# Attention scores on half the array's rows: two heads' products side by side, and one store of seven PSUM banks

## The chip, the core and the metric

The kernel runs on one core of a Trainium2 chip. The engines are PE (matrix products; PEld is its weight load), DVE (vector), ACT (scalar functions), POOL (general) and SP (issues the transfers). PE multiplies through an array of 128 rows and 128 columns: a weight block lies in the array, and the moving operand's columns stream through it. PE writes only to PSUM, which has eight banks of 512 float32 columns for each of 128 partitions; DVE and ACT read it from there. The metric is the device time of one execution in microseconds (us).

## What is computed

One transformer block, 2048 positions, width 512: a layer norm modulated by a conditioning vector, attention with 32 heads of 16 in a causal window of 256, a gated residual, a second layer norm, and a gated feed-forward part of 1792.

```python
def _A_ref(x, wqkv, wo):
    H = 32; Dh = D // H; W = 256
    ...
    scores = jnp.einsum("bhqd,bhkd->bhqk", q, k) * (Dh ** -0.5)
    mask = (idx[:, None] - idx[None, :] >= 0) & (idx[:, None] - idx[None, :] < W)
    scores = jnp.where(mask[None, None], scores, -1e9)
    p = _softmax(scores, axis=-1)
    o = jnp.einsum("bhqk,bhkd->bhqd", p, v)
    return (lambda x, *d: x.transpose(*d))(o, 0, 2, 1, 3).reshape(B, S, D) @ wo
...
h = _layernorm(x, axis=-1) * (1 + ca) + sa
x = x + ga * _A_ref(h, A_wqkv, A_wo)
h = _layernorm(x, axis=-1) * (1 + cb) + sb
x = x + gb * _B_ref(h, B_w1, B_w3, B_w2)
```

## The kernel before

Attention is cut into 32 units: 8 groups of four heads times 4 blocks of 512 positions. Unit u goes through three stages, which run at the same time for different units.

- `unit_a` (L429) projects queries and keys: 12 products of 512 columns into one bank (L438), two copies out of it on ACT (L444, L447), the rest on POOL (L451), and then SP spreads the rows into two rings, `ringk` and `ringq` (L457, L459). Numbers are kept in two parts, a coarse float32r one and its remainder, so that a head has 3 x 16 = 48 rows.
- `unit_b` (L475) finds each query's greatest score: a product (L485), then on DVE a mask and a maximum in one instruction (L494), which a short instruction follows that reads the result out. The negated maxima, again in two parts (L502, L503), are turned on PE (L509), copied by ACT (L514) and stored by SP as two more rows of `ringq` (L517), so that the score products subtract them.
- `unit_c` (L724) computes the scores transposed, keys by queries (L752), masks them, takes exponentials on ACT into `pt`, and multiplies by the values (L720): four heads side by side, each in a quarter of the array's columns, into the bank `po`. The result is copied out (L814) and stored.

The score products go two heads at a time (`a` counts the pairs of a unit). A pair's two heads stand one below the other in 96 rows, and `ringq` holds zeros in the other head's rows, so that a product keeps the heads apart by its columns: the maximum's products take 64 queries of both heads against up to 320 keys (L485), the scores' products 128 keys against both heads' 256 queries of the two near blocks, and one more of 256 columns for the far block (L752). The edges of the window are masked in one of four ways, by a letter for each of the eight score blocks of a unit in `MODE` (`MODL` for the last three units): C merges the two edge blocks on DVE (L772), so that one exponential serves both and POOL cuts the halves apart (L779); D adds masks on DVE (L760); P copies the edges to SBUF on ACT (L784), masks them on POOL (L794) and takes the exponentials from there (L786, L798); E adds the masks by a product on PE (L755).

PSUM's banks are dealt out by name: three `mx` (maxima, turns), three `st` (scores), one `pj` (projections), one `po`.

The order of all instructions up to the time `TS` is fixed by the table `X`: each operation of a unit has a place in it, units are 8 apart, and `at` collects them to be sorted. Each engine carries out its instructions in that order and waits where an operand or a bank is not ready. From `TS` on the same list is mixed with the output projection's and the feed-forward part's operations by `Sched.deal` (L150). A prologue does the first norm, the values, three units' `unit_a` and two units' `unit_b` by the table `Y`.

## Time and profile before

| | us |
|---|---|
| median of 3 runs (lowest, highest) | 968.09 (966.83, 968.49) |
| the profiled execution | 967.35 |
| its span, first to last instruction | 965.6 |
| PE busy | 921.7 (95%) |
| DVE busy | 672.0 (70%) |
| ACT busy | 524.8 (54%) |
| POOL busy | 544.1 (56%) |

The span is 1.75 us shorter than the execution's time. The mean granted TensorE clock is 0.988. Busy shares are means over stages that are limited in different ways; views by stretch and by line are needed to read a change in one stage. A matmul's record reaches from its issue to its modelled end, and neighbours overlap, so what one costs PE is the distance between starts, not its length.

### The profile page before, as it was taken

How to read it: one execution, taken by the hardware profiler on the slowest of the kernel's cores; microseconds unless marked ns; L12 is line 12 of the kernel's file. 1: busy time of each engine (PE TensorE's matmuls, PEld its weight loads, DVE VectorE, ACT ScalarE, POOL GpSimd, SP SyncE). 2: the span in 40 equal slices, each digit the busy share in tenths (PEclk: the TensorE clock that was granted, in tenths of full speed). 3: DMA queues.
4: the chain of work that ended last, by engine and by line, in shares of the span. 5: the costliest groups of instructions: out<-in, count | busy, mean ns of one | idle time of the engine just before them, and what ended most of it. 6: DMA issues, size and time to landing. Idle time of an engine off the chain costs nothing.

```text
span 965.6 us, 16735 instructions
## 1 busy us (share of the span) xinstructions
PE 921.7 (95%) x5330; PEld 708.9 (73%) x5330; DVE 672.0 (70%) x1864; ACT 524.8 (54%) x1031; POOL 544.1 (56%) x691
## 2 busy tenths in 40 slices
PE   5999999999999999978987999999999999999998
PEld 2678677777777777755665878888888888888886
DVE  7575689898898989876568555675569645565455
ACT  3333677787877777764677654333455334433330
POOL 5221465676656665643665689986657446443420
...
GB/s 307 174 87 46 105 186 163 153 149 163 183 170 139 163 160 149 138 181 183 247 218 1 206 222 312 215 184 162 77 166 149 182 42 95 98 65 92 25 22 87
DMA packets 125020, 141.62 MB, mean 147 GB/s; under 512 B 60034, under 2 KB 72834, under 8 KB 124932
## 3 DMA queue, kind: packets, MB, share of 16 engines
...
q10 hardware_dynamic: 720, 1.05, 0.3%
...
## 4 chain that ended last, share of the span: by engine, by line
PE 82%; DVE 7%; ACT 3%; DMA 3%; issue 3%; SPq 1%; POOL 1%; DVEq 0%; POOLq 0%; ACTq 0%
PE mx L1375 12%; PE st L1375 12%; PE pj L438 9%; PE st L752 8%; PE mx L485 8%; PE po L720 8%; PE st L1468 7%; PE mx L1468 7%; PE pj L1375 4%; PE st L652 2%; PE pj L1468 2%; PE st L1113 1%; PE mx L1113 1%; DVE junk L494 1%; DMA wo<-wsum 1%
## 5 line engine op out<-in xcount | busy, mean ns | idle before, releaser
L494 DVE CUSTOM_DVE_ANT_0 junk<-mx,mskq 128x320 bf16<-128x320 f32 (+4 forms) x512 | 223.0, 465 | 37.9 <-PE mx L485 37.1
L967 POOL TENSOR_TENSOR w<-w,w 128x512 fp32r<-128x512 f32 (+2 forms) x56 | 106.8, 1924 | 117.5 <-ACT w L966 99.0
L485 PE MATMUL mx<-ringk,ringq 96*128 96x320 f32 (+4 forms) x512 | 153.8, 324 | 5.5 <-DMA ringq<-qk 3.0
L752 PE MATMUL st<-ringq,ringk 98*128 98x256 f32 (+1 forms) x528 | 141.4, 336 | 7.1 <-DVE st L772 3.1
L779 POOL TENSOR_SCALAR_AFFINE_SELECT pt<-pt 128x256 f32<-128x256 f32 x224 | 92.4, 412 | 88.3 <-ACT pt L767 80.7
L438 PE MATMUL pj<-hT,wq 128*128 128x512 f32 x384 | 132.3, 402 | 1.8 <-ACT wq L423 1.0
L485 PEld LDWEIGHTS mx<-ringk,ringq 96*128 96x128 f32 x512 | 97.8, 192 | 44.5 <-DVE mt L494 21.4
L767 ACT ACTIVATE pt<-st 128x512 f32<-128x512 f32 (+1 forms) x198 | 115.8, 587 | 25.9 <-DVE st L760 7.7
L752 PEld LDWEIGHTS st<-ringq,ringk 98*128 98x128 f32 x528 | 91.1, 193 | 22.0 <-ACT pt L767 5.4
L720 PE MATMUL po<-pt,vS 128*17 128x384 f32 (+2 forms) x1408 | 92.5, 392 | 2.8 <-ACT pt L767 1.5
L438 PEld LDWEIGHTS pj<-hT,wq 128*128 128x128 f32 x384 | 68.3, 191 | 10.2 <-ACT wq L423 1.4
L1375 PE MATMUL mx<-b,w 128*128 128x512 f32 x264 | 68.2, 397 | 6.0 <-ACT t L1409 5.7
L1406 DVE TENSOR_TENSOR t<-mx,t 128x512 f32<-128x512 f32 x48 | 33.0, 689 | 45.3 <-PE mx L1375 22.6
L1406 DVE TENSOR_TENSOR t<-st,t 128x512 f32<-128x512 f32 x48 | 33.1, 690 | 44.7 <-PE st L1375 25.0
L720 PEld LDWEIGHTS po<-pt,vS 128*17 128x17 f32 x1408 | 34.8, 98 | 39.4 <-issue 19.9
L1375 PEld LDWEIGHTS mx<-b,w 128*128 128x128 f32 x264 | 50.1, 191 | 17.2 <-ACT t L1409 6.0
L1446 ACT ACTIVATE wq<-g 128x512 fp32r<-128x512 f32 x28 | 17.7, 631 | 81.6 <-DVE g L1402 33.6
L772 DVE COPY_PREDICATED st<-later,st 128x256 f32<-128x256 uint8 x112 | 47.4, 423 | 18.7 <-PE st L752 16.2
L1375 PE MATMUL st<-b,w 128*128 128x512 f32 x240 | 60.3, 390 | 0.0
L794 POOL TENSOR_SCALAR_AFFINE_SELECT sm<-sm 128x256 f32<-128x256 f32 x109 | 42.6, 409 | 28.7 <-ACT sm L784 27.7
L760 DVE TENSOR_TENSOR st<-st,mskr 128x256 f32<-128x256 f32 x125 | 53.6, 429 | 7.0 <-PE st L752 5.8
L451 POOL TENSOR_TENSOR qk<-qkr,qk 128x512 fp32r<-128x512 f32 x32 | 42.2, 1320 | 25.8 <-ACT qk L447 25.8
...
## 6 DMA issues: line engine op xcount, KB each, us to landing
...
ringq<-qk SPq DMA_DIRECT2D x192, 64.0 KB
...
```

Source lines behind the costliest of these rows:

```text
L438: nc.tensor.matmul(v["ps"], WQ[g][w][:, n // 3], hTp(i, n // 3, b * BT, BT), start=(n == 0), stop=(n == 3 * KC - 1))
L485: nc.tensor.matmul(v[i][:, :n], both_queries(a, gs), keys(NS, a, (gs + 1) * HP - n, n), start=True, stop=True)
L494: nc.vector.tensor_tensor_reduce(out=junk[:, :n], in0=v[i][:, :n], in1=mskq[:, WK - n:], scale=1.0, scalar=-3e38, op0=ALU.add, op1=ALU.max ...
L720: nc.tensor.matmul(po[32 * i:32 * i + DH + 1, qb * P:(qb + nq) * P], vS[:, kb, 4 * g + i], pts[i // 2][:, i % 2, c0:c0 + nq], start=first, ...
L752: nc.tensor.matmul(o, keys(NM, a, kb * P, P), queries(a, q, n), start=q == lo, stop=not plus and q + n == hi, skip_group_check=True)
L760: nc.vector.tensor_tensor(out=ps, in0=ps, in1=mskk[:, p:p + 1].to_broadcast([P, 2, P]), op=ALU.add)
L767: nc.scalar.activation(held[u, j, a][:, :, :n], v[j, a, 0].rearrange("p (h q) k -> p h q k", h=2)[:, :, :n], AF.Exp, scale=SCALE)
L779: nc.gpsimd.affine_select(out=pt[:, :, 2 * m], in_=pt[:, :, 0], **w)
L967: sch.op(eng, lambda: on_eng(eng).tensor_tensor(out=lo(), in0=src(), in1=hi().bitcast(F32), op=ALU.subtract), 0.06 + 0.0024 * n if eng == ...
L1375: nc.tensor.matmul(ps(bk), WT[s, n][w][:, col], BB[t, k][r], start=start and c == 0, stop=stop and c == 5, skip_group_check=True)
L1406: return nc.vector.tensor_add(o, x, y)
L1468: nc.tensor.matmul(ps(bk), tiles[hk + (h,)][:, i * P:(i + 1) * P], w2_of(last, y, f), start=(m == 0), stop=(m == 5))
```

## The change

Each head now has 64 rows of the rings to itself: one head of a pair lies in rows 0 to 63 of the array, the other in rows 64 to 127. A product of one head uses its 64 rows alone, and each product of old becomes two, one for each half, which write to two banks. The maximum's product takes 128 queries of one head against up to 384 keys (L497 of the new kernel), the scores' product 128 keys against up to 384 queries, near and far blocks in one (L764). The maximum's row comes to lie at rows 31, 63, 95 and 127, where the key ring holds ones; since these rows take part in the maximum's product, zeros are written there first (`zrow`). Masks, merges and exponentials work on one head and all its blocks (`hh` counts the heads), where they worked on two heads and one or two blocks. `MODE` drops D, gains one P and one E, whose masking products become an operation of their own (`plus`, L773). The named banks `mx`, `st` and `pj` become one store of seven, `take` handing out the one that was given back first. The table `X`, and with it the whole order, is new.

```diff
-WK = 5 * HP
-X = dict(oa=-3.863, ob=1.029, wqk=(-0.858, 1.939, 10.434), pj=(0.286, 0.344, 0.878, 1.131, 3.631, 3.672,
-         3.878, 4.077, 4.364, 4.951, 5.551, 5.743), ev=(7.049, 6.063), mix=(8.982,), row=(9.561, 6.099, 6.443,
-         6.374, 9.289, 9.261, 10.681, 9.981, 10.464), mx=(6.98, 5.852, 5.041, 5.414, 2.887, 8.92, 4.178, 7.678,
-         8.523, 4.734, 2.476, 7.344, 4.677, 8.087, 3.397, 9.325), tl=(0.121, 1.116, 0.068, 0.241, 0.054, 0.054,
-         0.03, 0.054, 0.03, 0.429, 0.101, 0.086, 0.03, 0.03, 0.03, 0.03), mr=(10.275, 10.832, 11.16, 11.231),
-         st=(2.246, 2.098, 4.353, 2.468, 3.726, 3.854, 5.37, 5.955, 6.87, 6.701, 5.531, 6.783, 8.785, 8.433,
-         8.729, 8.272), c1=(0.082, 0.03, 0.03, 0.03, 0.58, 0.083, 0.104, 0.452), c2=(0.996, 0.977, 1.143, 0.243,
-         0.033, 0.569, 0.983, 0.032), c3=(0.25, 6.673, 0.348, 1.207, 1.713, 0.316, 0.385, 1.653), pv=(6.434,
-         10.575, 10.975, 11.087, 6.249, 6.261), o=(11.83, 12.324), job=(0.275, 3.004, 9.681), gate=7.93)
+WK = 3 * P
...
-MODE = 'CDCPCDCP'
...
+MODE = 'CPCPCPCE'
...
-MXB = 3
-STB = 3
-MODL = 'CECECECE'
+XN = 7
+MODL = 'CPCPCPCE'
 NL = 3
 XB = 6
-PTB = 9
+PTB = 12
...
+    free, gone, left = list(range(XN)), [], {}
+    def take(uses=1):
+        i = free.pop(0)
+        left[i] = uses
+        return i, psA.tile([P, BT], F32, name=f"x{i}", bufs=1)
+    def done(bank, give=0):
+        i = bank[0]
+        left[i] -= 1
+        if left[i] == 0:
+            if give or left.get("give"):
+                left["give"] = left.get("give", 0) + give - 1
+                gone.append(i)
+            else:
+                free.append(i)
...
-    ringq = ap.tile([P, NB, 2, 8, 2, HP], F32R, name="ringq")
-    NS, NM = 6 * DH, 6 * DH + 2
-    def queries(a, qb, n):
-        b, i = divmod(qb, 4)
-        return ringq[:NM, b, a, 2 * i:2 * (i + n)].rearrange("p s h t -> p h s t")
-    def both_queries(a, qs):
-        return ringq[:NS, qs // 8, a, qs % 8].rearrange("p h t -> p (h t)")
-    def keys(rows, a, lo, n):
-        return ringk[:rows, a, lo:lo + n]
+    ringq = ap.tile([P, 2, S], F32R, name="ringq")
+    zrow = ap.tile([4, 2, BT], F32, name="zrow")
+    nc.gpsimd.memset(zrow, 0.0)
+    sel = ap.tile([P, 5], F32, name="sel")
+    nc.gpsimd.memset(sel, 0.0)
+    nc.gpsimd.affine_select(out=sel[:, :4], in_=sel[:, :4], pattern=[[-32, 4]], base=-31, channel_multiplier=1,
+                            compare_op=ALU.not_equal, fill=1.0)
+    def hrow(ring, hh, a, lo, n):
+        return ring[HP * hh:HP * hh + HP, a, lo:lo + n]
...
-            (r, low), n = ((((0, 0), 0), ((1, 2), 0), ((2, 1), 1))[n // 3], n % 3)
-            raw = v[low].bitcast(F32)
-            if n == 0:
-                nc.sync.dma_start(ringk.bitcast(F32)[r[0]:NS:3, :, b * BT:(b + 1) * BT], raw[:HP])
-            else:
-                nc.sync.dma_start(
-                    ringq.bitcast(F32)[NS // 2 * (n - 1) + r[1]:NS // 2 * n:3, b, :, :, n - 1].rearrange(
-                        "p a s t -> p (a s) t"),
-                    raw[HP + 32 * (n - 1):HP + 32 * n])
+            if n == 6:
+                nc.sync.dma_start(ringq.bitcast(F32)[31::32, :, b * BT:(b + 1) * BT], zrow)
+                return
+            (r, low), n = ((((0, 0), 0), ((1, 2), 0), ((2, 1), 1))[n // 2], n % 2)
+            ring = (ringk, ringq)[n].bitcast(F32)
+            nc.sync.dma_start(ring[r[n]::4, :, b * BT:(b + 1) * BT], v[low].bitcast(F32)[HP * n:HP * n + HP])
...
-            qs, a = divmod(i, 2)
-            gs = 8 * b + qs
-            n = min(5, gs + 1) * HP
-            v[i] = psA.tile([P, BT], F32, name="mx", bufs=MXB)
-            nc.tensor.matmul(v[i][:, :n], both_queries(a, gs), keys(NS, a, (gs + 1) * HP - n, n),
-                             start=True, stop=True)
-        def top(i):
-            qs, a = divmod(i, 2)
-            n = min(5, 8 * b + qs + 1) * HP
+            qb, a = divmod(i, 2)
+            q = 4 * b + qb
+            n = min(3, q + 1) * P
+            for hh in range(2):
+                v[i, hh] = take()
+                nc.tensor.matmul(v[i, hh][1][:, :n], hrow(ringq, hh, a, q * P, P),
+                                 hrow(ringk, hh, a, (q + 1) * P - n, n), start=True, stop=True)
+        def top(i, hh):
+            qb, a = divmod(i, 2)
+            n = min(3, 4 * b + qb + 1) * P
             if "mt" not in v:
-                v["mt"] = a1.tile([P, 2, 8], F32, name="mt", bufs=2)
+                v["mt"] = a1.tile([P, 4, 4], F32, name="mt", bufs=2)
             junk = a1.tile([P, WK], BF16, name="junk", bufs=2)
             nc.vector.tensor_tensor_reduce(
-                out=junk[:, :n], in0=v[i][:, :n], in1=mskq[:, WK - n:], scale=1.0, scalar=-3e38,
-                op0=ALU.add, op1=ALU.max, accum_out=v["mt"][:, a, qs:qs + 1])
+                out=junk[:, :n], in0=v[i, hh][1][:, :n], in1=mskq[:, WK - n:], scale=1.0, scalar=-3e38,
+                op0=ALU.add, op1=ALU.max, accum_out=v["mt"][:, 2 * a + hh, qb:qb + 1])
+            done(v[i, hh])
...
+        def rows(a):
+            nc.sync.dma_start(ringq.bitcast(F32)[31::32, a, b * BT:(b + 1) * BT], v["mT"][16 * a:16 * a + 16])
...
-        def bank(j, a, p):
-            ps = v[j, a, p]
-            return ps.rearrange("p (h q) k -> p h q k", h=2)[:, :, 0] if p == 0 else ps[:, :2]
-        def scores(j, a, p):
-            kb = 4 * b + j
+        def scores(j, a):
+            kb, n = 4 * b + j, blocks(j)
             if (u, j, a) not in held:
                 held[u, j, a] = a2.tile([P, 2, 3, P], F32, name="pt", bufs=PTB)
-            v[j, a, p] = ps = psA.tile([P, 4, P], F32, name="st", bufs=STB)
-            plus = mode(j, a) == "E"
-            lo, hi = (kb, kb + min(2, blocks(j))) if p == 0 else (kb + 2, kb + 3)
-            both = [(lo, hi - lo)] if lo // 4 == (hi - 1) // 4 else [(lo, 1), (hi - 1, 1)]
-            for q, n in both:
-                o = ps.rearrange("p (h q) k -> p h q k", h=2)[:, :, q - lo:q - lo + n] if p == 0 else ps[:, :2]
-                nc.tensor.matmul(o, keys(NM, a, kb * P, P), queries(a, q, n), start=q == lo,
-                                 stop=not plus and q + n == hi, skip_group_check=True)
-            if plus:
-                nc.tensor.matmul(bank(j, a, p), identr, mskr[:, p:p + 1].to_broadcast([P, 2, P]), start=False,
+            for hh in range(2):
+                v[j, a, "b", hh] = take()
+                v[j, a, hh] = ps = v[j, a, "b", hh][1].rearrange("p (q k) -> p q k", k=P)
+                nc.tensor.matmul(ps[:, :n].rearrange("p q k -> p (q k)"), hrow(ringk, hh, a, kb * P, P),
+                                 hrow(ringq, hh, a, kb * P, n * P), start=True,
+                                 stop=mode(j, a) != "E", skip_group_check=True)
+        def edge(t, j):
+            return t[:, 0:3:2] if blocks(j) == 3 else t[:, :1]
+        def plus(j, a):
+            for hh in range(2):
+                nc.tensor.matmul(edge(v[j, a, hh], j), identr, mskr[:, :2 if blocks(j) == 3 else 1], start=False,
                                  stop=True, skip_group_check=True)
-        def mask(j, a, p):
-            ps = bank(j, a, p)
-            nc.vector.tensor_tensor(out=ps, in0=ps, in1=mskk[:, p:p + 1].to_broadcast([P, 2, P]), op=ALU.add)
-        def probs(j, a, p):
-            n = min(2, blocks(j))
-            if p:
-                nc.scalar.activation(held[u, j, a][:, :, 2], bank(j, a, 1), AF.Exp, scale=SCALE)
-            else:
-                nc.scalar.activation(held[u, j, a][:, :, :n], v[j, a, 0].rearrange(
-                    "p (h q) k -> p h q k", h=2)[:, :, :n], AF.Exp, scale=SCALE)
-        def merge(j, a):
-            nc.vector.copy_predicated(bank(j, a, 0), later, bank(j, a, 1))
+        def mask(j, a, hh):
+            ps = edge(v[j, a, hh], j)
+            nc.vector.tensor_tensor(out=ps, in0=ps, in1=mskk[:, :2 if blocks(j) == 3 else 1], op=ALU.add)
+        def probs(j, a, hh):
+            n = 2 if mode(j, a) == "C" else blocks(j)
+            nc.scalar.activation(held[u, j, a][:, hh, :n], v[j, a, hh][:, :n], AF.Exp, scale=SCALE)
+            done(v[j, a, "b", hh])
+        def merge(j, a, hh):
+            ps = v[j, a, hh]
+            nc.vector.copy_predicated(ps[:, 0], later, ps[:, 2])
...
-        def side(j, a, p):
+        def side(j, a, hh):
             if (j, a, "m") not in v:
-                v[j, a, "m"] = a2.tile([P, 2, 2, P], F32, name="sm", bufs=1)
-            nc.scalar.activation(v[j, a, "m"][:, :, p], bank(j, a, p), AF.Copy)
-            if p == 0 and blocks(j) > 1:
-                nc.scalar.activation(held[u, j, a][:, :, 1], v[j, a, 0].rearrange(
-                    "p (h q) k -> p h q k", h=2)[:, :, 1], AF.Exp, scale=SCALE)
+                v[j, a, "m"] = a2.tile([P, 2, 2, P], F32, name="sm", bufs=2)
+            ps = v[j, a, hh]
+            nc.scalar.activation(v[j, a, "m"][:, hh, :2 if blocks(j) == 3 else 1], edge(ps, j), AF.Copy)
+            if blocks(j) > 1:
+                nc.scalar.activation(held[u, j, a][:, hh, 1], ps[:, 1], AF.Exp, scale=SCALE)
+            done(v[j, a, "b", hh])
```

PE's order in the middle of the attention loop, before: rows of one unit, from a visit of the value products (L720) on; L485 is a maximum's product, L752 a score's, L438 a projection's, L509 the turn.

```order
L720 MATMUL po<-pt,vS 17x384 x4
L720 MATMUL po<-pt,vS 17x256 x4
L720 MATMUL po<-pt,vS 17x128 x4
L485 MATMUL mx<-ringk,ringq 128x320
L752 MATMUL st<-ringq,ringk 128x512
L752 MATMUL st<-ringq,ringk 128x256
L509 MATMUL mx<-ident,mr 32x128
L485 MATMUL mx<-ringk,ringq 128x320
L752 MATMUL st<-ringq,ringk 128x512
L438 MATMUL pj<-hT,wq_2190 128x512
L485 MATMUL mx<-ringk,ringq 128x320
L438 MATMUL pj<-hT,wq_2190 128x512
```

The same place in the new order, with the numbers of banks and tiles; L497 is a maximum's product on half the rows, L764 a score's, L773 the masking product of mode E, L451 a projection's, L740 a value product.

```order
L497 MATMUL x2_2304<-ringk_103,ringq_104 128x384
L497 MATMUL x6_2306<-ringk_103,ringq_104 128x384
L764 MATMUL x4_2309<-ringq_104,ringk_103 128x384
L764 MATMUL x1_2311<-ringq_104,ringk_103 128x384
L773 MATMUL x4_2309<-mskr_129,identr_130 128x2x128
L773 MATMUL x1_2311<-mskr_129,identr_130 128x2x128
L451 MATMUL x0_2291<-hT_95,wq00_1509 128x512
L497 MATMUL x3_2319<-ringk_103,ringq_104 128x384
L497 MATMUL x5_2321<-ringk_103,ringq_104 128x384
L740 MATMUL po_99<-pt_2165,vS_101 17x384 x2
L740 MATMUL po_99<-pt_2223,vS_101 17x384 x2
L497 MATMUL x2_2330<-ringk_103,ringq_104 128x384
```

Before, products on the whole array stood one behind the other, and the value products' quarters came in long visits; now pairs on half the rows stand between single whole-array products and short visits.

DVE's order in the loop, before: L494 is the maximum (and the row that reads it out), L772 a merge, L760 a mask.

```order
L494 ISA junk_5365,mt_5364<-mx_5360,mskq_105 128x320
L494 ISA mt_5364 128x1
L772 COPY_PREDICATED st_5368<-later_127,st_5372 128x2x128
L494 ISA junk_5379,mt_5364<-mx_5377,mskq_105 128x320
L494 ISA mt_5364 128x1
L760 TENSOR_TENSOR st_5385<-st_5385,mskr_128 128x2x128
L494 ISA junk_5392,mt_5364<-mx_5390,mskq_105 128x320
```

And now, where L506 is the maximum and L788 a merge:

```order
L506 ISA junk_5762,mt_5723<-x2_5758,mskq_112 128x384
L506 ISA mt_5723 128x1
L506 ISA junk_5764,mt_5723<-x0_5760,mskq_112 128x384
L506 ISA mt_5723 128x1
L788 COPY_PREDICATED x5_5782<-later_128,x5_5782 128x128
L506 ISA junk_5814,mt_5723<-x1_5786,mskq_112 128x384
L506 ISA mt_5723 128x1
L788 COPY_PREDICATED x6_5784<-later_128,x6_5784 128x128
```

The maxima grew from 320 to 384 columns, a merge of two heads became two of one head, and the masks are gone from this place.

157 lines of the change are left out of this document (90 added, 67 removed).

## The prediction

> **What bounds the kernel now.** The first view is the busy time of each engine in stretches of the span (columns: microseconds of the stretch, then busy time of PE, PE's weight loads, DVE, ACT and POOL, the granted clock, the DMA share). The rows are the attention loop, the tail in which attention runs out under the output projection, and most of the feed-forward part; a prologue lies ahead.
>
> ```profile
> core 0 of [0], span 965.6 us
> ...
> 136.00:414.00 278.00, 276.30 (x2249) 204.14 (x2241) 246.84 (x1043) 212.08 (x485) 178.27 (x347) 1.00 0.60 156
> 414.00:480.00 66.00, 55.21 (x370) 36.66 (x362) 41.80 (x118) 36.33 (x78) 31.89 (x47) 0.92 0.73 202
> ...
> 520.00:966.00 446.00, 439.85 (x1910) 357.20 (x1910) 261.84 (x366) 182.76 (x290) 253.86 (x190) 0.99 0.40 130
> ```
>
> From 136 to 414 us PE is busy 276.3 of 278 us at full clock; DVE has 89%, ACT 76%, POOL 64%. The next view groups that stretch's instructions by line and shape (busy time, mean of one).
>
> ```profile
> L494 DVE CUSTOM_DVE_ANT_0 junk<-mx,mskq 128x320 bf16<-128x320 f32 x352 | 161.1, 485 | 18.9 <-PE mx L485 18.2
> L485 PE MATMUL mx<-ringk,ringq 96*128 96x320 f32 x352 | 106.7, 328 | 0.0
> L438 PE MATMUL pj<-hT,wq 128*128 128x512 f32 x300 | 101.6, 399 | 0.0
> ...
> L752 PE MATMUL st<-ringq,ringk 98*128 98x256 f32 x258 | 61.5, 289 | 0.0
> L752 PE MATMUL st<-ringq,ringk 98*128 98x512 f32 x150 | 55.5, 397 | 0.0
> ...
> L760 DVE TENSOR_TENSOR st<-st,mskr 128x256 f32<-128x256 f32 x107 | 45.9, 429 | 4.6 <-PE st L752 3.6
> L720 PE MATMUL po<-pt,vS 128*17 128x384 f32 x400 | 41.8, 490 | 0.0
> L772 DVE COPY_PREDICATED st<-later,st 128x256 f32<-128x256 uint8 x86 | 36.4, 424 | 2.6 <-PE st L752 2.0
> L794 POOL TENSOR_SCALAR_AFFINE_SELECT sm<-sm 128x256 f32<-128x256 f32 x93 | 36.3, 408 | 25.3 <-ACT sm L784 24.4
> ...
> L720 PE MATMUL po<-pt,vS 128*17 128x256 f32 x356 | 27.4, 379 | 0.0
> ...
> L720 PE MATMUL po<-pt,vS 128*17 128x128 f32 x360 | 18.3, 275 | 0.0
> ...
> L444 ACT ACTIVATE qkr<-pj 128x512 f32<-128x512 f32 x25 | 14.9, 596 | 0.0
> ```
>
> L444 runs once per unit (a head group's block), so these are 25 units of **11.12 us**. Means of one overlap; what an instruction costs its engine is the distance to the next start, read from PE's timeline (start, length, engine, line; x2 merges two neighbours).
>
> ```profile
> 299.94 0.63 PE L438 MATMUL pj<-hT,wq 128*128 128x512 f32 x2
> 300.41 0.31 PE L485 MATMUL mx<-ringk,ringq 96*128 96x320 f32 x1
> 300.56 0.52 PE L752 MATMUL st<-ringq,ringk 98*128 98x256 f32 x2
> 300.91 0.31 PE L485 MATMUL mx<-ringk,ringq 96*128 96x320 f32 x1
> 301.06 0.28 PE L752 MATMUL st<-ringq,ringk 98*128 98x256 f32 x1
> 301.27 1.49 PE L720 MATMUL po<-pt,vS 128*17 128x384 f32 x24
> 302.69 0.41 PE L485 MATMUL mx<-ringk,ringq 96*128 96x320 f32 x1
> 302.94 0.51 PE L752 MATMUL st<-ringq,ringk 98*128 98x512 f32 x2
> 303.29 0.27 PE L509 MATMUL mx<-ident,mr 128*32 128x128 f32 x1
> 303.32 0.33 PE L485 MATMUL mx<-ringk,ringq 96*128 96x192 f32 x1
> 303.49 0.42 PE L752 MATMUL st<-ringq,ringk 98*128 98x512 f32 x1
> ```
>
> The weight loads at the values, from the same view:
>
> ```profile
> 301.27 0.13 PEld L720 LDWEIGHTS po<-pt,vS 128*17 128x17 f32 x8 [0.17 <-POOL pt L779]
> 301.61 0.12 PEld L720 LDWEIGHTS po<-pt,vS 128*17 128x17 f32 x4 [0.20 <-issue]
> 301.93 0.55 PEld L720 LDWEIGHTS po<-pt,vS 128*17 128x17 f32 x12 [0.21 <-issue]
> ```
>
> A 512-column product costs 0.235 us (two from 299.94 to 300.41), a 320-column one 0.15: 0.44 ns a column, so 256 columns 0.12 and 384 columns 0.18. Four value products on the four column quarters run together: one pass of 384 columns by all four takes 0.33 (weight loads at 301.27, 301.61, 301.93), two passes make a call, and 256 or 128 columns in proportion 0.22 and 0.11. A visit to these quarters has a price besides: the 256-column product ahead of it takes 0.21 in place of 0.12; the 24 records take 1.42 where their passes, 2 x (0.33 + 0.22 + 0.11), make 1.32; the product behind takes 0.25 in place of 0.15, its weights being late. That is 0.3 us a visit. The turn at 303.29, 32 columns wide, pays none: it and the 192-column product (0.09) take 0.20 together.
>
> The PE sum over 25 units: products 300 x 0.235 = 70.5; maxima 352 x 0.15 + 3.7 for the 48 shorter ones = 56.5; scores 150 x 0.235 + 258 x 0.115 = 65; values 100 x 0.33 + 89 x 0.22 + 90 x 0.11 = 62.5; turns 2.8; two visits a unit 15. Together 272 of 278, 10.9 us a unit: PE's own work sets the period, with 0.2 us of waits.
>
> **The change on PE.** A unit had 16 maximum products and about 16 score products, each over nearly the whole array. Now it has 16 pairs of 384 columns, each product on 64 rows. If a pair's halves run together, it costs 0.18; four units hold 60 pairs of 384, two of 256 and two of 128, so 2.8 a unit where (56.5 + 65)/25 = 4.9 stood. Products stay at 2.8, values at 2.5, the turn at 0.1; the new mask products of mode E add two of 256 columns, 0.2. The new order visits the column quarters 3.7 times a unit, not twice: 1.1. Sum: **9.5**, 1.4 less than before.
>
> The unknown is the step between products on all rows and pairs on halves: the new order has 331 of them in 28 units, 11.8 a unit, and no row shows one. The two nearest rows disagree. By the turn it costs nothing; by the values' visit it costs 0.09 to empty the array and 0.10 for weights that could not be loaded ahead, 0.2 each, 2.4 a unit. It decides the sign: at (10.9 - 9.5)/11.8 = 0.12 us a step the whole gain is gone. I take nothing, since a pair, like the turn, still fills the columns in one go from adjoining rows, and keep 0.2 as the other end; I hold this choice loosely.
>
> By the Trainium skill's "TensorEngine Tiling (Array Packing)", section Tiling Modes, changing the tiling mode, not just the tile, drains the engine. The visits of the values agree with that, 0.3 us each, and the turn does not; by the rule the sum would be that of the dear step below.
>
> **The change on the other engines.** Costs again from start to next start, on DVE and then on ACT.
>
> ```profile
> 300.43 0.49 DVE L494 CUSTOM_DVE_ANT_0 junk<-mx,mskq 128x320 bf16<-128x320 f32 x1
> ...
> 300.85 0.49 DVE L494 CUSTOM_DVE_ANT_0 junk<-mx,mskq 128x320 bf16<-128x320 f32 x1
> ...
> 301.26 0.42 DVE L772 COPY_PREDICATED st<-later,st 128x256 f32<-128x256 uint8 x1
> 301.59 0.48 DVE L494 CUSTOM_DVE_ANT_0 junk<-mx,mskq 128x320 bf16<-128x320 f32 x1
> ...
> 303.89 0.35 DVE L494 CUSTOM_DVE_ANT_0 junk<-mx,mskq 128x192 bf16<-128x192 f32 x1
> 304.17 0.43 DVE L760 TENSOR_TENSOR st<-st,mskr 128x256 f32<-128x256 f32 x1
> 304.50 0.48 DVE L494 CUSTOM_DVE_ANT_0 junk<-mx,mskq 128x320 bf16<-128x320 f32 x1
> ```
>
> ```profile
> 302.12 0.61 ACT L767 ACTIVATE pt<-st 128x512 f32<-128x512 f32 x1
> 302.59 0.41 ACT L765 ACTIVATE pt<-st 128x256 f32<-128x256 f32 x1
> 302.86 0.64 ACT L814 ACTIVATE os<-po 128x512 f32<-128x512 f32 x1
> ```
>
> DVE before: maxima 352 x 0.41 and 48 shorter ones, 6.25 a unit; masks 107 x 0.33, 1.4; merges 86 x 0.33, 1.1; the two halves of the maximum some 0.65: 9.4. After: 64 columns more are 0.065 more by the 320 and 192 rows, so 0.475 a maximum and 7.2 a unit; the masks all but go (0.2); seven merges of 128 columns at 0.33 - 0.13 = 0.2 make 1.4; 0.65 stays. Together 9.45, **the same**. ACT: mode D's exponentials go (107 pieces at 0.27 to 0.47 over 25 units, -1.6); one more block takes mode P, with two copies at 0.27, two short exponentials at 0.16 and one of 512 columns at 0.5, +1.4; E brings two of 384 columns, +0.7; D's remainder and C's exponential in two parts, +0.4. That is 0.9 on 212/25 = 8.5: 9.4. POOL: mode P's selections go from 93 in 25 units to 5.75 a unit, +2 x 0.39 on 7.1: 7.9. On SP nine 64-column query and key issues become seven with whole rows, and the maximum's one issue becomes two; PE's waits for DMA are not among the terms above, so this counts as nothing, and if the rows came late, the first maximum of a unit would show it.
>
> One store of seven banks serves 34 uses a unit; at 10.2 us a use can keep its bank 7 x 10.2/34 = 2.1 us. Before, three banks served 16 maxima and a turn in 11.12: 2.0. So the banks are about as short as they were; no term.
>
> **The sum.** PE 9.5, DVE 9.45 and ACT 9.4 now stand side by side. One bound left 0.2 of waits; with three I take 0.7: period **10.2** (bounds: 9.7 with the waits of before, 10.7 with twice my value). The loop counts 28 units, 25 in the quoted stretch, two ahead of it and one behind: 28 x (11.12 - 10.2) = 25.8. Two units' maxima lie in the prologue: 2 x (2.3 - 1.4) = 1.8. In the tail PE idles 11 of 66 us, so less PE work there buys nothing that I count (-5 to +3). The feed-forward part is untouched. The profiled execution took 967.35, so 967.35 - 27.6 = 939.8; the median of the runs is 0.7 higher: **940**, and 926 to 954 with the period's bounds.
>
> **Rivals.** *A small step*: only the emptying, 0.09 a step, 1.06 a unit: 10.6 + 0.25 of waits, (11.12 - 10.85) x 28 + 1.8 = 9.4, **959**. For it: weights of pairs may be loaded ahead, as they are ahead of the turn.
>
> *A dear step, slower*: 0.2 a step. PE 9.5 + 2.4 = 11.9, period 12.1, +27.4 - 1.8: **994**. It decides from 0.12 us a step on. For it: every visit of the values pays its price, on both sides. Against it: the turn at 303.29.
>
> *The halves don't run together*: the second product of a pair has a bank of its own to wait for, and may start when the first is done. All of them: 9.5 + 2.8 + 0.2, 12.5 a unit, 1005; half of them: 9.5 + 1.4 + 0.2, 11.1, 966. Against it: the four quarters of the value products do start together (8 loads within 0.13 us at 301.27), and the banks are no shorter than before. The Trainium skill's "TensorE: Matmul & The Clock Gate", Part 3, says that products on distinct row groups run concurrently, with starts about 4 ns apart; the value products' column quarters agree, and no run here shows rows.
>
> **How the numbers follow.** Forecast 0.42, small step 0.18, dear step 0.26, halves apart 0.10, and 0.04 for the rest, such as late rows or a tail that takes the gain back. About 0.2% is what a measurement of this kernel can tell from no change. Faster: the first two, 0.60. Within 0.2%: 0.05, out of halves apart and the seam between small and dear. Slower: 0.35. For 8 in 10 the range must reach the dear step's centre and a little beyond: 926 to 996; left out are its upper part, half of the halves apart, and less than 926. The forecast's own range is 926 to 954.
>
> **What would show it.** Right: 64-row products in pairs that start within some 10 ns; a period of 9.7 to 10.7; DVE above 92% busy in the loop; no gap ahead of a weight load where the rows change. Wrong: 0.1 to 0.2 us between a pair and a full product and a period above 11.1 with PE full (dear step); starts of a pair 0.18 apart (halves apart); PE waiting at a unit's first maximum for DMA (late rows).

## The result, and the profile after

| | before | after |
|---|---|---|
| median of 4 runs each (lowest, highest), us | 968.29 (966.83, 971.17) | 996.54 (993.41, 997.03) |
| ratio, 95% interval | | 1.028 [1.025, 1.031] |
| the profiled execution, us | 967.35 | 996.35 |
| first copy of `os`, of the 28th, of the 32nd, end of span, us | 114.0, 414.3, 471.5, 965.6 | 119.2, 440.9, 500.0, 994.5 |

The change makes the kernel 2.8% slower. The forecast was 940; the time is that of the rival called the dear step (994). `os` is copied once a unit, so its starts are the attention loop's clock: of the 29 us, 5 are there before the first copy, 21 come in the loop (27 units of 11.91 us where 11.12 stood), 2 in the last four units and under 1 behind them.

Busy time by stretch, after (columns as before: stretch, PE, weight loads, DVE, ACT, POOL, clock, DMA share):

```profile
core 0 of [0], span 994.5 us
...
136.00:414.00 278.00, 278.00 (x2121) 135.50 (x2120) 232.00 (x979) 219.78 (x683) 185.53 (x373) 1.00 0.55 151
```

PE has no gap left in these 278 us: the trace shows it waiting neither for banks nor for late rows, and every other engine has time to spare: DVE 83%, where the forecast needed 92% or more. So PE is what got slower, though it streams fewer columns. The groups of that stretch:

```profile
L506 DVE CUSTOM_DVE_ANT_0 junk<-x,mskq 128x384 bf16<-128x384 f32 x330 | 170.6, 555 | 30.4 <-PE x L497 26.2
L451 PE MATMUL x<-hT,wq 128*128 128x512 f32 x280 | 103.1, 447 | 0.0
L497 PE MATMUL x<-ringk,ringq 64*128 64x384 f32 x330 | 72.1, 428 | 0.0
...
L764 PE MATMUL x<-ringq,ringk 64*128 64x384 f32 x326 | 59.5, 371 | 0.0
```

DVE's maxima now wait 26 us for PE. One record of a projection's product (L451) has grown from 399 to 447 ns, though nothing in it changed: its neighbours did. PE's timeline shows how (start, length, engine, line; x2 of L497 or L764 is a pair, x8 of L740 two passes of values):

```profile
300.00 1.20 PE L451 MATMUL x<-hT,wq 128*128 128x512 f32 x4
301.13 0.45 PE L497 MATMUL x<-ringk,ringq 64*128 64x384 f32 x2
301.41 0.34 PE L764 MATMUL x<-ringq,ringk 64*128 64x384 f32 x2
301.68 0.51 PE L773 MATMUL x<-mskr,identr 128*128 128x256 f32 x2
302.02 0.39 PE L451 MATMUL x<-hT,wq 128*128 128x512 f32 x1
302.34 0.44 PE L497 MATMUL x<-ringk,ringq 64*128 64x384 f32 x2
302.71 0.84 PE L740 MATMUL po<-pt,vS 128*17 128x384 f32 x8
303.48 0.44 PE L497 MATMUL x<-ringk,ringq 64*128 64x384 f32 x2
303.76 0.33 PE L764 MATMUL x<-ringq,ringk 64*128 64x384 f32 x2
304.02 0.49 PE L451 MATMUL x<-hT,wq 128*128 128x512 f32 x1
304.45 0.45 PE L764 MATMUL x<-ringq,ringk 64*128 64x384 f32 x2
304.82 0.50 PE L451 MATMUL x<-hT,wq 128*128 128x512 f32 x1
```

A pair's two products do run together: both are over in 0.34 to 0.45 us, as one alone is (a run below shows one), and in the trace their starts lie 3 to 4 ns apart in most pairs. But each change between products of all rows and pairs costs on both sides. Ahead of it PE loses 0.09, which the prediction read as the array emptying: the product at 302.02 takes 0.32 to the next start in place of 0.235, the pair at 301.41 takes 0.27 in place of 0.18. Behind it 0.10 is lost, since the second set of weights is late: pair to pair from 301.13 takes 0.28, the two mask products from 301.68 take 0.34 in place of 0.235. The weight loads of this stretch (PEld) fit that:

```profile
301.13 0.19 PEld L497 LDWEIGHTS x<-ringk,ringq 64*128 64x128 f32 x2 [0.37 <-DVE mt L506]
301.24 0.19 PEld L764 LDWEIGHTS x<-ringq,ringk 64*128 64x128 f32 x2
301.68 0.30 PEld L773 LDWEIGHTS x<-mskr,identr 128*128 128x128 f32 x2 [0.25 <-issue]
301.91 0.19 PEld L451 LDWEIGHTS x<-hT,wq 128*128 128x128 f32 x1
```

The first load behind a change starts together with its own product (301.13, 301.68), not ahead of it; the load for the product at 302.02, with no change before it, starts 0.11 ahead. A pair or a product that stands alone pays both: 302.34 takes 0.37, 304.02 takes 0.43. From 301.13 to 304.82 are 3.69 us; the columns in it need 6 x 0.18 + 3 x 0.235 + 0.66 = 2.45 (the two mask products count as one of 512), and seven changes share the other 1.24: **0.18 each**. It is the price of the values' visits, 0.09 and 0.10. Not every difference in rows counts: in the kernel before, products on 96, 98 and 128 rows followed each other without it (0.15 and 0.235 in the prediction's rows).

Summed like this over the 21 or 22 units between the copies of `os` from 150 to 410 us (distance to the next start, less 0.45 ns a column, 0.86 in the values' passes), PE streams for 8.0 us a unit where it streamed for 10.0, as the change intends, and loses 3.8 beside that where it lost 1.1; 3.6 and 0.6 of these lie at products next to a change. The one gains 2.0 us, the other takes 2.7.

### The profile page after: what moved, and what is told of

Its sections match the earlier page's. It is cut to its first block, busy times and chain, and to the rows that moved or that the text cites. A ratio compares the mean times of both kernels' runs of the same rounds, so it can differ in the third digit from the quotient of the medians.

```text
span 994.5 us, 17565 instructions
## 1 busy us (share of the span) xinstructions
PE 954.3 (96%) x5356; PEld 632.6 (64%) x5356; DVE 675.1 (68%) x1884; ACT 556.4 (56%) x1354; POOL 568.0 (57%) x763
## 4 chain that ended last, share of the span: by engine, by line
PE 81%; DMA 6%; DVE 5%; POOL 3%; ACT 3%; issue 2%; SPq 0%; POOLq 0%; DVEq 0%; ACTq 0%
PE x L1402 25%; PE x L1495 16%; PE x L451 12%; PE po L740 8%; PE x L497 8%; PE x L764 6%; PE x L671 4%; PE x L773 1%; DMA ringk<-qk 1%; DMA x1a<-in_x 1%; DVE b L1299 1%; DVE t L1291 1%; DMA o_dr<-os 1%; DMA wq<-o_dr 1%; DMA vS<-in_wmod 1%
## 5 line engine op out<-in xcount | busy, mean ns | idle before, releaser
L506 DVE CUSTOM_DVE_ANT_0 junk<-x,mskq 128x384 bf16<-128x384 f32 (+2 forms) x512 | 251.9, 529 | 64.5 <-PE x L497 59.2
L1433 DVE TENSOR_TENSOR t<-x,t 128x512 f32<-128x512 f32 x112 | 77.1, 689 | 108.0 <-PE x L1402 56.3
L451 PE MATMUL x<-hT,wq 128*128 128x512 f32 x384 | 142.8, 445 | 1.8 <-ACT wq L436 1.4
L1402 PE MATMUL x<-b,w 128*128 128x512 f32 x588 | 137.0, 390 | 0.9 <-DVE t L1433 0.9
L782 ACT ACTIVATE pt<-x 128x256 f32<-128x256 f32 (+2 forms) x320 | 109.5, 384 | 40.7 <-DVE x L788 15.8
L1402 PEld LDWEIGHTS x<-b,w 128*128 128x128 f32 x588 | 110.1, 188 | 24.5 <-DVE t L1433 1.3
L497 PE MATMUL x<-ringk,ringq 64*128 64x384 f32 (+2 forms) x512 | 112.0, 426 | 9.3 <-DMA ringk<-qk 8.1
L740 PE MATMUL po<-pt,vS 128*17 128x384 f32 (+2 forms) x1408 | 108.8, 404 | 3.9 <-ACT pt L815 2.2
L497 PEld LDWEIGHTS x<-ringk,ringq 64*128 64x128 f32 x512 | 50.5, 187 | 85.5 <-issue 42.5
L764 PE MATMUL x<-ringq,ringk 64*128 64x384 f32 (+2 forms) x512 | 95.9, 378 | 2.3 <-DMA ringq<-mT 1.3
L451 PEld LDWEIGHTS x<-hT,wq 128*128 128x128 f32 x384 | 66.0, 189 | 43.5 <-issue 25.5
L801 ACT ACTIVATE sm<-x 128x256 f32<-128x256 f32 x192 | 72.9, 380 | 29.7 <-PE x L764 28.8
L764 PEld LDWEIGHTS x<-ringq,ringk 64*128 64x128 f32 x512 | 50.2, 192 | 48.7 <-ACT pt L803 20.3
L1495 PE MATMUL x<-w,wq 128*128 128x512 f32 x336 | 80.2, 394 | 0.0
L788 DVE COPY_PREDICATED x<-later,x 128x128 f32<-128x128 uint8 x224 | 54.4, 290 | 25.4 <-PE x L764 20.9
```

Source lines behind the costliest of these rows:

```text
L451: nc.tensor.matmul(v["ps"][1], WQ[g][w][:, n // 3], hTp(i, n // 3, b * BT, BT), start=(n == 0), stop=(n == 3 * KC - 1))
L497: nc.tensor.matmul(v[i, hh][1][:, :n], hrow(ringq, hh, a, q * P, P), hrow(ringk, hh, a, (q + 1) * P - n, n), start=True, stop=True)
L506: nc.vector.tensor_tensor_reduce(out=junk[:, :n], in0=v[i, hh][1][:, :n], in1=mskq[:, WK - n:], scale=1.0, scalar=-3e38, op0=ALU.add, op1= ...
L740: nc.tensor.matmul(po[32 * i:32 * i + DH + 1, qb * P:(qb + nq) * P], vS[:, kb, 4 * g + i], pts[i // 2][:, i % 2, c0:c0 + nq], start=first, ...
L764: nc.tensor.matmul(ps[:, :n].rearrange("p q k -> p (q k)"), hrow(ringk, hh, a, kb * P, P), hrow(ringq, hh, a, kb * P, n * P), start=True, ...
L782: nc.scalar.activation(held[u, j, a][:, hh, :n], v[j, a, hh][:, :n], AF.Exp, scale=SCALE)
```

## The experiments

The theory that came out of this: a step between array modes costs 0.2 us, and the steps are the whole loss. Rivals: the seven banks are what holds the loop (34 uses a unit), or DVE's maxima, or late rows. All runs are compared with runs of the kernel before on the same chip; those of before, after, e4, e5 and e9 were repeated, the others were run once, and the four runs of the changed kernel spread over 3.6 us. Periods are from the first and last copy of `os` between 150 and 410 us (190 to 450 in the two runs whose clock was low before that). Steps are counted in PE's order over 28 units, to pairs and to the values together; 209 of the changed kernel's 540 are its visits to the values. The 781 of e2 are counted over the whole kernel.

| run | steps | period, us | time, us |
|---|---|---|---|
| before / after | 109 / 540 | 11.14 / 11.89 | 968.3 / 996.5 |
| e2_maxima_64_rows | 109 + 781 | 15.68 | 1119.8 |
| e3_plain_turn | 109 + turns | 11.48 | 976.9 |
| e1_full_rows | 209 | 10.70 | 955.2 |
| e13_full_rows_banks_withheld | 209 | 11.51 | 981.3 |
| e16_full_rows_banks_as_dealt | 209 | 10.68 | 961.0 |
| e17_half_rows_one_bank | 540 | 11.79 | 1011.4 (low clock) |
| e11_changed_short_maxima | 540 | 11.87 | 999.6 |
| e6_values_gathered | 480 | 12.06 | 1016.6 |
| e7_projections_gathered | 426 | 11.79 | 989.3 |
| e9_runs_of_two_pairs | 426 | 11.86 | 1004.5 |
| e5_gathered_short_runs | 368 | 11.65 | 1000.1 |
| e4_gathered | 314 | 12.28 | 1018.9 |
| e10_projections_gathered_short_maxima | 426 | 11.72 | 986.4 |
| e15_full_rows_banks_withheld_gathered | 207 | 11.90 | 993.8 |
| e18_half_rows_one_bank_gathered | 426 | 11.43 | 1008.1 (low clock) |

### The price of one step

The kernel before, its maxima on 64 of the 96 rows (SCALE is 1e-3 here too):

```diff
-        return ringq[:NS, qs // 8, a, qs % 8].rearrange("p h t -> p (h t)")
+        return ringq[:HP, qs // 8, a, qs % 8].rearrange("p h t -> p (h t)")
...
-            nc.tensor.matmul(v[i][:, :n], both_queries(a, gs), keys(NS, a, (gs + 1) * HP - n, n),
+            nc.tensor.matmul(v[i][:, :n], both_queries(a, gs), keys(HP, a, (gs + 1) * HP - n, n),
```

> The kernel before with the maximum's products on the first 64 of their 96 rows (one third of the contraction is left out, and the exponential's scale made small); nothing else changes. There are 435 runs of maxima among other products, so 870 edges, 89 of them at a visit of the values, which was paid before: 781 new steps. Theory (any step between a product on half the rows and one on all rows costs 0.2 us): +156, time 1090 to 1130. Rival (only two halves with weights of their own make a step dear): 965 to 975.

It took 1119.75, 151 more: 0.19 us for each of 781 steps. PE's timeline of this run:

```profile
301.81 0.41 PE L485 MATMUL mx<-ringk,ringq 64*128 64x320 f32 x1
302.15 0.50 PE L752 MATMUL st<-ringq,ringk 98*128 98x512 f32 x1
302.58 0.41 PE L485 MATMUL mx<-ringk,ringq 64*128 64x320 f32 x1
302.92 0.50 PE L438 MATMUL pj<-hT,wq 128*128 128x512 f32 x1
```

The maximum of 320 columns takes 0.34 where it took 0.15, the score product 0.43 where it took 0.235. No pair, no second bank and no new order is in this kernel, so the price belongs to the change between 64 rows and more, itself.

The prediction had chosen zero because the turn, a product of 32 columns, paid nothing. The turn is a transposing product; the next kernel makes it a plain one with the identity.

```diff
-            nc.tensor.transpose(v["tp"][:32, :P],
-                                v["mr"].bitcast(F32).rearrange("p l m -> p (l m)"), ident)
+            nc.tensor.matmul(v["tp"][:32, :P], v["mr"].bitcast(F32).rearrange("p l m -> p (l m)"), ident,
+                             start=True, stop=True)
```

> The kernel before with the turn as a plain product with the identity in place of a transposing one, same shape (128 rows, 32 columns), same result. The turn of before paid nothing for its 32 columns. Theory (a transposing product doesn't count as a change of the array's division, a plain one of the same shape does): the turn and the product behind it take 0.5 us or more together, where they took 0.20; 32 turns, time 974 to 984. Rival (a single product on few columns is free in any form): 0.2 to 0.35 us together, time 966 to 972.

It took 976.88, 8 more, and the period grew by 0.34. PE's timeline of this run:

```profile
308.13 0.51 PE L752 MATMUL st<-ringq,ringk 98*128 98x512 f32 x2
308.56 0.41 PE L509 MATMUL mx<-ident,mr 128*32 128x128 f32 x2
308.90 0.35 PE L485 MATMUL mx<-ringk,ringq 96*128 96x192 f32 x1
309.09 0.42 PE L752 MATMUL st<-ringq,ringk 98*128 98x512 f32 x1
```

The turn and the 192-column product behind it take 0.53 where they took 0.20. Part of that is not a step: the plain product needs two passes, 0.13 apart in the trace. The rest, 0.2 here and 0.09 ahead of it, is what the values' visits pay. So the turn was free as a transposing product, not because it fills the columns in one go: the same 32 columns pay when the product is plain. For a pair's change it was the wrong row to take the price from.

### Steps or banks

The changed kernel with one product of 128 rows for each pair: no step to half rows is left, and half the banks are in use.

```diff
-            for hh in range(2):
-                v[i, hh] = take()
-                nc.tensor.matmul(v[i, hh][1][:, :n], hrow(ringq, hh, a, q * P, P),
-                                 hrow(ringk, hh, a, (q + 1) * P - n, n), start=True, stop=True)
+            v[i, 0] = v[i, 1] = take(2)
+            nc.tensor.matmul(v[i, 0][1][:, :n], ringq[:, a, q * P:q * P + P],
+                             ringk[:, a, (q + 1) * P - n:(q + 1) * P], start=True, stop=True)
...
-SCALE = DH ** -0.5
+SCALE = 1e-3
```

(and the scores' products likewise)

> The changed kernel with one product on all 128 rows in place of each pair; both heads' readers read its one bank (a pair's two heads are summed into one, the exponential's scale is made small, so the output is another one). PE's columns, the order and the work of DVE, ACT, POOL and SP stay; the steps between half rows and all rows are gone. Theory (the steps cost the time): the period falls from 11.9 to 9.6 to 10.4 us a unit, time 935 to 955. Rival (the longer maxima, ACT's added work or late rows hold the period, and PE only looks full): the period stays above 11.3, time above 980.

955.23, 41 less than the changed kernel, at the upper end of what was expected (the period, 10.70, is 0.3 beyond its 10.4). But two things had gone, the steps and half the bank uses. The next kernel withholds a second bank for each pair:

```diff
+            v[i, "d"] = hold()
...
+            if hh:
+                done(v[i, "d"])
```

> As the run with one product of all 128 rows for each pair (numbers of both heads are mixed, SCALE is 1e-3), but each pair also withholds a second bank from the store, as long as its first, so that the seven banks go round as fast as in the changed kernel: no step between array modes, the changed kernel's banks. Theory (the steps hold the changed kernel up): period 10.6 to 11.0, 952 to 968. Rival (the run with one bank for each pair was fast since a pair took half the banks): period over 11.4, 980 or more.

981.27: the theory's expectation failed, the rival's was met. But this kernel gives its first bank of a pair back one reader later than the changed kernel does. So the last of this kind deals the banks in exactly the changed kernel's order:

```diff
+            v[i, "d"] = hold()
+            v[i, 0] = v[i, 1] = take()
...
-            done(v[i, hh])
+            done(v[i, hh if hh else "d"])
```

> As the run with full rows and banks withheld (one product of 128 rows a pair, numbers of both heads mixed, SCALE 1e-3), but the withheld bank is given back when its reader of the first head is done, as the changed kernel gives back its own, so that the banks are dealt exactly as there and none is given back later. No steps. Theory (the seven banks alone hold the kernel at about 11.4, steps or none): period 11.2 to 11.6, 968 to 985. Rival (the run before was slow only because its banks came back late): period 10.9 or less, 965 or less.

960.98, period 10.68, as with half the banks: this time the rival was right, which puts the run before down to its late return. One caution: only the second bank of a pair is really waited for here, since nothing is written to the withheld one, so part of the difference may be a wait that this run leaves out. The counterpart has all steps and half the banks:

```diff
-            for hh in range(2):
-                v[i, hh] = take()
-                nc.tensor.matmul(v[i, hh][1][:, :n], hrow(ringq, hh, a, q * P, P),
-                                 hrow(ringk, hh, a, (q + 1) * P - n, n), start=True, stop=True)
+            v[i, 0] = v[i, 1] = take(2)
+            nc.tensor.matmul(v[i, 0][1][:, :n], hrow(ringq, 0, a, q * P, P),
+                             hrow(ringk, 0, a, (q + 1) * P - n, n), start=True, stop=True)
```

> The changed kernel with the second head's products left out: each pair is one product of 64 rows, both heads' readers read its bank, so that half the banks are used; SCALE is 1e-3. PE's order and its 540 steps are as in the changed kernel. Theory (the steps alone set 11.9, whatever the banks): period 11.6 to 11.9, 983 to 997. Rival (the banks set it): period 11.2 or less, 975 or less.

The period was 11.79 from 198 us on, as the theory has it; ahead of that the granted clock was low, so the whole time (1011) says nothing. The copies of `os` (count, shortest/median/longest in ns, first to last start), of after, of full rows with the banks as dealt, and of half rows with half the banks:

```profile
L831 ACT ACTIVATE os<-po x22: 597/598/602, 155.2 to 404.9; 128x512 f32<-128x512 f32 x22
```

```profile
L836 ACT ACTIVATE os<-po x24: 575/586/601, 159.2 to 404.8; 128x512 f32<-128x512 f32 x24
```

```profile
L829 ACT ACTIVATE os<-po x22: 575/597/597, 197.7 to 445.3; 128x512 f32<-128x512 f32 x22
```

That is 249.7/21 = 11.89, 245.6/23 = 10.68 and 247.6/21 = 11.79. Steps there or not make 1.1 to 1.2 us a unit, half the banks or all at most 0.1. So **the steps set the changed kernel's period, the banks don't**, though a bank that comes back one reader later costs up to 0.8 as soon as the steps are gone. PE's timeline in the run with full rows and banks as dealt, and in the run with half rows and one bank:

```profile
300.92 0.34 PE L502 MATMUL x<-ringk,ringq 128*128 128x384 f32 x1
301.09 1.10 PE L456 MATMUL x<-hT,wq 128*128 128x512 f32 x4
```

```profile
303.91 0.44 PE L496 MATMUL x<-ringk,ringq 64*128 64x384 f32 x1
304.19 0.34 PE L762 MATMUL x<-ringq,ringk 64*128 64x384 f32 x1
304.45 0.49 PE L451 MATMUL x<-hT,wq 128*128 128x512 f32 x1
304.88 0.44 PE L496 MATMUL x<-ringk,ringq 64*128 64x384 f32 x1
```

With all rows a maximum of 384 columns is followed after 0.17 by a product; on half rows, even without a partner, 0.28, 0.26 and 0.43 stand where the changed kernel has 0.28, 0.26 and 0.43.

DVE is excluded by maxima over 128 columns in the changed kernel:

```diff
-                out=junk[:, :n], in0=v[i, hh][1][:, :n], in1=mskq[:, WK - n:], scale=1.0, scalar=-3e38,
+                out=junk[:, :P], in0=v[i, hh][1][:, n - P:n], in1=mskq[:, WK - P:], scale=1.0, scalar=-3e38,
```

> The changed kernel with each maximum taken over 128 of its up to 384 columns (the others are left out, and SCALE is 1e-3). Theory (PE with its steps sets the period, DVE waits beside it): DVE's busy time falls by a third or more, the time by less than 1%: 985 to 997, period 11.7 to 11.9. Rival (the maxima on DVE are what the changed kernel waits for): under 975.

999.59, period 11.87: nothing gained, as the theory has it (one run, 2.6 us outside the expected 997), though DVE is busy for 147 of 278 us where it was for 232.

### Fewer steps

If a step costs 0.2 us, an order with fewer steps should win. PE's order alone was changed, by the times of projections (`pj`) and values (`pv`) in `X`. The first order gathers both:

```diff
-X = dict(oa=-3.211, ob=-2.53, wqk=(2.274, 2.575, 11.003), pj=(-0.348, -0.299, -0.287, -0.279, -0.049,
-         0.096, 0.42, 0.443, 1.122, 1.228, 1.512, 2.913), ev=(5.9, 5.248), mix=(7.349,), row=(9.442, 6.888,
+X = dict(oa=-3.211, ob=-2.53, wqk=(2.274, 2.575, 11.003), pj=(-0.348, -0.299, -0.287, -0.279, -0.074,
+         -0.073, -0.072, -0.071, 1.45, 1.451, 1.512, 1.513), ev=(5.9, 5.248), mix=(7.349,), row=(9.442, 6.888,
...
-         0.058, 0.03, 0.03, 0.298, 0.03), pv=(4.755, 5.472, 7.243, 7.388, 2.508, 3.161), o=(7.473, 10.163),
+         0.058, 0.03, 0.03, 0.298, 0.03), pv=(5.471, 5.472, 7.387, 7.388, 3.16, 3.161), o=(7.473, 10.163),
```

> The changed kernel with another order on PE alone: projections gathered into three runs a unit, value products into three visits. Steps between half rows and all rows fall from 331 to 163 in 28 units, visits from 104 to 75. Theory (0.2 us a step, 0.3 a visit): (168 x 0.2 + 29 x 0.3)/28 = 1.5 us a unit less, period 10.4, time 955; up to 970 where a run of six pairs waits for banks. Rival (order does not matter, DVE or ACT hold the period): 990 or more.

1018.88, ratio to before 1.051 [1.046, 1.056]: 49 us above the expected range, and in the wrong direction. The rival's bound is met, but not its reason, that order does not matter: this order costs 22 us. Six pairs now follow each other. PE's timeline of this run:

```profile
300.56 0.61 PE L497 MATMUL x<-ringk,ringq 64*128 64x384 f32 x4
301.02 0.28 PE L764 MATMUL x<-ringq,ringk 64*128 64x256 f32 x2
301.69 0.87 PE L764 MATMUL x<-ringq,ringk 64*128 64x256 f32 x2 [0.40 <-DVE mt L506]
302.27 0.81 PE L497 MATMUL x<-ringk,ringq 64*128 64x384 f32 x2
302.75 0.81 PE L764 MATMUL x<-ringq,ringk 64*128 64x384 f32 x2
```

The first three pairs take six of seven banks. The fourth waits 0.40 for a maximum to be read, and from there on the halves come apart: 0.81 to 0.87 a pair, where a pair in step has 0.28 to 0.45. In the loop 75 of 364 pairs start over 50 ns apart, in the changed kernel 12 of 374. Next, four projections go into the middle of that run; after it the values alone (the `pv` line of the diff above), and the projections alone (the `pj` lines of this one):

```diff
-X = dict(oa=-3.211, ob=-2.53, wqk=(2.274, 2.575, 11.003), pj=(-0.348, -0.299, -0.287, -0.279, -0.049,
-         0.096, 0.42, 0.443, 1.122, 1.228, 1.512, 2.913), ev=(5.9, 5.248), mix=(7.349,), row=(9.442, 6.888,
+X = dict(oa=-3.211, ob=-2.53, wqk=(2.274, 2.575, 11.003), pj=(-0.348, -0.299, -0.287, -0.279, 0.096,
+         0.097, 0.098, 0.099, 1.45, 1.451, 1.512, 1.513), ev=(5.9, 5.248), mix=(7.349,), row=(9.442, 6.888,
...
-         0.058, 0.03, 0.03, 0.298, 0.03), pv=(4.755, 5.472, 7.243, 7.388, 2.508, 3.161), o=(7.473, 10.163),
+         0.058, 0.03, 0.03, 0.298, 0.03), pv=(5.471, 5.472, 7.387, 7.388, 3.16, 3.161), o=(7.473, 10.163),
```

> The changed kernel with PE's order alone changed, as in the run before it that gathered the projections and the value visits, but with four of the projections put into the middle of the long run of six pairs, so that no run has more than three pairs (six of the seven banks). Steps in the loop 540 -> 368 (between products of all rows and pairs 331 -> 217, visits to the values' array 209 -> 151). Theory (a step costs 0.2 us; the run before was slow since its long run of pairs found no free banks and the halves came apart, 75 of 364 pairs against 12 of 374): 172 x 0.2 = 34 us less than the changed kernel, 958 to 972, period 10.6 to 11.1, fewer than 25 pairs apart. Rival 1 (gathering is dear by itself, since projections and value products come too late or too early for their readers): 1000 or more, few pairs apart. Rival 2 (steps are not what sets the time once they are few; DVE, ACT and the banks do, as period 10.7 without any step suggests): 975 to 990 with PE waiting for maxima or banks at other places.

> The changed kernel with the visits to the values alone gathered, 104 -> 76 in the loop, the products left where they are. Steps 540 -> 480; the longest run of pairs has three. Theory (0.2 us a step): 12 us less than the changed kernel, 980 to 990, period 11.4 to 11.6. Rival 1 (gathering is dear by itself): no gain or slower, 996 or more.

> The changed kernel with the projections alone gathered, four, four and two and two around the turn, the value visits left where they are. Steps 540 -> 426; the longest run of pairs has three. Theory (0.2 us a step): 23 us less than the changed kernel, 968 to 980, period 11.0 to 11.3. Rival 1 (gathering is dear by itself): no gain or slower, 996 or more. Rival 2 (other bounds take over): 982 to 992.

They took 1000.14 (ratio 1.032 [1.029, 1.034]), 1016.62 and 989.3, and 48 of 382, 35 of 370 and 66 of 378 pairs came apart. The first meets rival 1's time, but not its few pairs apart. Only gathering the projections gained, 7 us in place of 23, as rival 2 (other bounds take over) had it. The pairs apart are such a bound: their second halves start, summed, 0.61 us a unit behind the first, in the changed kernel 0.14, while 114 steps at 0.19 are 0.77 a unit. Gathering the values lost 20, as rival 1 had it: from the last copy of `os` to the end took 505.8 us in place of 494.5, the first copy came 4.8 later, and the loop was slower too. In all four orders that move the values' visits that last part is 10 to 13 us longer (494.9 with the projections alone); why was not followed up. The step's price itself shows again where a run of three finds its banks free; PE's timeline with the projections gathered:

```profile
305.20 0.44 PE L764 MATMUL x<-ringq,ringk 64*128 64x384 f32 x2
305.48 0.34 PE L497 MATMUL x<-ringk,ringq 64*128 64x384 f32 x2
305.65 0.34 PE L764 MATMUL x<-ringq,ringk 64*128 64x384 f32 x2
305.93 0.52 PE L740 MATMUL po<-pt,vS 128*17 128x384 f32 x4
```

The second pair comes 0.28 after the first, the third 0.17 after the second: weights are late once a change, not once a pair. So runs of exactly two, eight a unit:

```diff
-X = dict(oa=-3.211, ob=-2.53, wqk=(2.274, 2.575, 11.003), pj=(-0.348, -0.299, -0.287, -0.279, -0.049,
-         0.096, 0.42, 0.443, 1.122, 1.228, 1.512, 2.913), ev=(5.9, 5.248), mix=(7.349,), row=(9.442, 6.888,
+X = dict(oa=-3.211, ob=-2.53, wqk=(2.274, 2.575, 11.003), pj=(-0.348, -0.299, -0.287, -0.279, 0.42,
+         0.421, 0.422, 0.443, 1.45, 1.451, 1.512, 1.513), ev=(5.9, 5.248), mix=(7.349,), row=(9.442, 6.888,
...
-         0.058, 0.03, 0.03, 0.298, 0.03), pv=(4.755, 5.472, 7.243, 7.388, 2.508, 3.161), o=(7.473, 10.163),
+         0.058, 0.03, 0.03, 0.298, 0.03), pv=(4.8475, 5.472, 7.403, 7.404, 3.16, 3.161), o=(7.473, 10.163),
```

> The changed kernel with PE's order alone changed so that every run of pairs has two: projections four, four and two and two around the turn, two of the value visits moved past one pair each. Steps in the loop 540 -> 426, as in the run that gathered the projections, but without its runs of three. Theory (0.2 us a step, and gathering pays in full only while banks are free for the pairs): 114 x 0.2 = 23 us less than the changed kernel, 970 to 980, period 11.0 to 11.3, halves apart in fewer than 25 pairs. Rival (moving the value visits is dear by itself, as the run that gathered them alone was): 990 or more.

1004.53, ratio 1.038 [1.035, 1.042], slower again, as the rival had it; 505.6 us of it lie behind the last copy, and the loop gains nothing either (11.86), with 30 of 374 pairs apart. Then the projections gathered, with the maxima over 128 columns of the diff above, to see whether the banks wait for DVE:

> The run with the projections alone gathered, with each maximum taken over 128 of its up to 384 columns (the others are left out, and SCALE is 1e-3), so that DVE empties a bank in about half the time. Theory (the gathered kernels lose to late banks what they save in steps): the halves that start apart fall from 66 to under 15, period 11.0 to 11.3, 968 to 978, a gain over the same kernel with whole maxima at least 8 us greater than the changed kernel's own gain from short maxima. Rival (the order itself, not the banks, is dear): the two kernels gain alike from short maxima.

986.39, 2.9 less than with whole maxima, no more than runs of one kernel spread, and 60 of 381 pairs still apart: shorter maxima don't help, so this theory fell. Does the order cost something where there are no half rows at all? The first run with banks withheld, in that order (the same `pj` lines):

> The same with the order of the run that gathered the projections alone. Neither kernel has a step between modes, so what differs is the order against banks, DVE and ACT. Theory (gathering gave back most of its saved steps because pairs that follow each other find banks not yet read): this one is slower than its ungathered twin by 4 to 20 us. Rival (gathering saved so little because a step costs less there than 0.2 us): within 3 us of its twin.

993.75, 12.5 more than its twin, as expected: the same move costs 0.4 us a unit where it saves no step, at least in a kernel that gives its banks back late. And with half the banks free, the run with half rows and one bank in that order (again the `pj` lines):

> The same with the projections gathered (steps 540 -> 426). With banks to spare, gathering should pay in full: theory (0.2 us a step) 18 to 28 us less than its ungathered twin, period 0.65 to 1.0 less. Rival (a step costs little in this kernel, gathered or not): a gain under 10 us.

The period was 11.43 where its twin had 11.79: 0.36 a unit, 10 us in 28 units, just at the rival's bound and half of what the theory wanted. The busy times by stretch, of the twin and of this run:

```profile
190.00:450.00 260.00, 259.40 (x1659) 126.38 (x1658) 225.61 (x925) 204.73 (x644) 175.32 (x357) 1.00 0.55 151
```

```profile
194.00:446.00 252.00, 245.52 (x1672) 124.55 (x1665) 219.74 (x928) 204.37 (x646) 175.94 (x358) 1.00 0.57 156
```

PE's gaps grow from 0.6 to 6.5 us, 0.3 us a unit: most of what is missing has become waiting. 4.2 us of these gaps end when the maximum's rows land (`ringq`), 2.0 when `os` has been copied out of `po`. So gathering saves its steps and loses them to waits: with all banks in use to halves that come apart, with half of them free to rows and copies whose place in the order stayed as it was. Which of DVE's and ACT's places would have to move along was not tried, and no order tried comes below the kernel before.

## Why the prediction was wrong

**The step that failed** is the price of a change of rows: "I take nothing, since a pair, like the turn, still fills the columns in one go from adjoining rows". It is 0.19 us (781 of them in the kernel before) or 0.18 (seven in a row of the changed kernel's timeline), the other end of the range given. Of the two rows that disagreed the wrong one was followed: the turn is exempt because it transposes, which its plain version shows, and the values' visit was the neighbour. The rival's sum, 9.5 + 11.8 x 0.2 = 11.9 a unit, is what PE takes, 11.9; its 0.2 of waits on top are not there, as PE has no gap. That the rival's 994 is so close to 996.5 is in part luck: the loop came out some 6 us shorter than its sum, the prologue 7 and the last units 2 longer. The prediction's own bound, 0.12 us a step, from which the change loses, was passed. The rule of the Trainium skill's "TensorEngine Tiling (Array Packing)", section Tiling Modes, that changing the mode drains the engine, agrees with the 0.09 ahead of each change. The 0.10 for weights behind it is as dear and is not in that sentence.

**Halves together**: right, 3 to 4 ns apart in the trace; 12 of 374 pairs were not. That is also what the Trainium skill's "TensorE: Matmul & The Clock Gate", Part 3, says of distinct row groups.

**PE without its steps**: right in kind. PE streams 2.0 us a unit less. But the period without steps to half rows is 10.68, not 10.2, and the kernel 961, not 940. PE's own sum holds: in that run it streams 8.1 a unit and its visits cost 1.5, 9.6 together. With PE, DVE and ACT side by side I took 0.7 of waits; the other 1.1 are waits and small losses. 17 of 278 us are plain gaps, of which 8 end with DVE's reading of a bank and 5 with rows that land late; the rest is inside PE's records and was not taken apart. So even with a free step the forecast was 20 us too good.

**Banks as short as before, no term**: right for the changed kernel, whose period hardly moves with half of them free (11.79 for 11.89); wrong as a margin, since one later return cost up to 0.8 a unit, and every gathered order that uses all banks has more pairs apart (30 to 75 of some 370).

**DVE the same, ACT and POOL up**: of no consequence. DVE is 83% busy and gained nothing from shorter maxima.

**The prologue's two units**, forecast at -1.8, came to +5.2, of which 3.0 go with the steps to half rows (first copy at 116.2 without them); the rest was not followed up. **The tail**: 2 more, within its bounds.
